# Row-reversing copies of two outputs in a single-core forward and backward kernel: three large DMAs against sixteen small ones

## The chip, the cores and the metric

The kernel runs on one core of one Trainium2 chip. The metric is device time in microseconds (us) of one launch, forward and backward together. A core has a matrix engine (TensorE, PE in the profile), VectorE (DVE), ScalarE (ACT), GpSimd (POOL) and SyncE (SP); each runs its own instructions in order, and DMAs are issued by SP, ACT or POOL and then run by themselves. An engine waits on semaphores, so an instruction that waits also holds up what stands behind it on its engine.

## The reference, cut to what matters

```python
def _fwd_reference(A_u, ..., B_w1, B_w3, B_w2):
    x  = A_u                                   # 1 x 2048 x 576, bf16
    xn = _layernorm(x)
    # s: a state-space convolution along the 2048 rows
    K  = einsum("dn,dnl,dn->dl", C, exp(dt * A * l), dt * B).real
    s  = irfft(rfft(xn, padded to 2L) * rfft(K, padded to 2L))[:L] + xn * Dskip
    # g: a gated MLP, width 4608
    g  = silu((silu(xn @ w1) * (xn @ w3)) @ w2)
    return x + s * g

def reference(..., grad_out):
    out, vjp = jax.vjp(_fwd_reference, ...)
    return (out, *vjp(grad_out))   # out, dA_u, eight gradients of the
                                   # state-space parameters, dw1, dw3, dw2
```

out_0 is `out` and out_1 is the gradient of A_u, each 2048 x 576 in bf16. out_10, out_11 and out_12 are the gradients of the three weight matrices.

## The kernel before, in words

**Token tiles.** The 2048 rows are worked in 16 tiles of 128 rows. The convolution is done with matrix products that play the part of Fourier transforms, and for these the odd tiles hold their rows in reversed order. `self.order` (in `backward`) lists the eight odd tiles first, then the eight even ones. A result of an even tile goes straight to its place in the output. A result of an odd tile goes to a scratch tensor in DRAM, `self.odd["out_0"]` or `self.odd["out_1"]`, 8 x 128 x 576 each, 1152 KB. From there DMAs from DRAM to DRAM copy it to the output with the rows turned round again; the helper `turned` (L173) gives the access pattern of the odd rows of an output in reversed order.

**Stages around the change.** The forward stage ends with the stores of out_0 and of its odd tiles (L1152). Then `ssm_bwd_conv` (L1183) runs the backward of the convolution in four quarters (`conv_bwd_quarter`), interleaved with the weight gradients of the MLP. These are worked in 18 groups of 256 columns: `backward` loops over `gi` and takes each group's generator, `phase6_group` (L1724), stage by stage. In a group, matmuls L1746 make `ph`, ACT casts it to `gh` (L1749), DVE multiplies `gu_n` and `gg_n` by it (L1764), SP stores both to `GU_dram` and `GG_dram` (L1769, two halves each), and L1807 to L1822 make the gradients of w1 and w3, which POOL stores (L1792, L1813). ACT's Silu and its derivative for the next group are L1713 and L1717, with DVE's products L1720 and L1721. Stages named "out_11_0" to "out_10_1" are steps of the gradient part, "stored" comes right behind the stores.

In a convolution quarter, SP loads spectra (L86: `a` from `UH_dram` and `KH_dram`, `az` likewise), DVE multiplies them with `g` to `Z` and `ZZ` (L867 to L876, L1319, L1324), TensorE turns these back (L841, L851), ACT evicts `gds_sb` and `gk_st` (L1332, L1337, L1340), and SP stores them (L1334, L1344).

**The last stage** (`phase6_inputs`) runs over the 16 tiles in `self.order`, i = 0 to 15. For each, SP loads transposed activations `acts` from `GU_dram` and `GG_dram` (L1669), TensorE multiplies them with the weights (`px`, L1857), and `ln_bwd_tile` and `ln_finish` do the backward of the layer norm (L1896 to L1931) and store the tile. Between these, the parameter gradients take `gz` and `pz` (L1376, L1379) and a transposed `qT` (L1669, from `Q_dram`) through matmuls L1389, DVE's product `pr_q` (L1394) and its sum (L1397).

**What sets the order.** The program is written as generators with due times: `self.at(T)` sets a priority, and a scheduler then arranges each engine's instructions by these priorities and by an estimate of when operands are ready. `issue_after(x)` makes an instruction be issued behind x. The helper `self.sp` keeps a class of SP's DMAs in the order in which they are written. So a moved DMA can also move instructions of other engines.

**The copies.** out_0 is one DMA of 8 x 128 x 576 on SP's queue at L1200, due at `T0 + 60`. out_1 is two DMAs of 4 x 128 x 576 on POOL's queue at L1934, written behind the finish of tiles i = 10 and i = 13, and set by the scheduler at 1553 and 1645 us of the profiled execution.

Of the kernel before, what the change touches and what calls it, by code (L numbers as in the profile page):

```python
# [100 lines left out]
class K:  # L101
# [71 lines left out]
    def turned(self, ap, t0=0, t1=None):  # L173
        rows = ap.rearrange("(i two p) d -> two i p d", two=2, p=P)[1]
        return rows[t0:t1, ::-1]

    def tok(self, name, t):
        ap = self.aps[name].flatten_outer_dims()
# [1004 lines left out]
    def ssm_bwd_conv(self, T0, TQ, ps):  # L1183
        nc, cfg = self.nc, self.cfg
        D, LT = cfg.D, cfg.LT
        self.gK_dram = self.dram.tile([4, P // 2, D // 64, 2, 2, 2, 8 * LT], BF16, name="gK_dram")
        with self.pool(name="b_g", bufs=1, side="right") as self.bgp, \
                self.pool(name="b_k", bufs=1, side="right") as kp, self.pool(name="b_z", bufs=2, side="right") as zp:
            self.at(T0)
            self.lcol = kp.tile([P, LT], FP32, name="lcol")  # L1190
            nc.vector.tensor_scalar(out=self.lcol[:], in0=self.irow[:, 0:LT], scalar1=float(P),
                                    scalar2=self.pcol[:, 0:1], op0=ALU.mult, op1=ALU.add)
            nc.vector.tensor_scalar(out=self.lcol[:], in0=self.lcol[:], scalar1=1.0 / 512, scalar2=None, op0=ALU.mult)
            self.at(T0 - 100)
            self.dft_turn_sines()
            self.cCS = kp.tile([P, 2, 2, cfg.LS], BF16, name="cCSb")
            with self.tc.issue_after(self.hc_loads[5].ins):
                nc.sync.dma_start(out=self.cCS[:], in_=self.CS_dram[:].rearrange("m i p k -> p m i k"))
            self.at(T0 + 60)
            nc.sync.dma_start(out=self.turned(self.aps["out_0"].flatten_outer_dims()), in_=self.odd["out_0"][:])  # L1200
            for g in range(4):
                yield from self.conv_bwd_quarter(g, kp, zp, ps, T0 + g * TQ, TQ)

# [306 lines left out]
    def backward(self, T0, TG, TQ, TC, TX, gctx, mats):  # L1510
        nc, cfg = self.nc, self.cfg
# [11 lines left out]
        with ExitStack() as out:  # L1523
# [60 lines left out]
            for gi in range(NG):  # L1584
                self.chain = gi >= GP
                lastg = gi == NG - 1
                nxt = self.phase6_load(gi + 1, T0 + TG * gi, TG, wp, inp) if not lastg else None
                prep = nxt[-1] if nxt else iter(())
                if lastg:
                    self.tail()  # L1590
                self.at(T0 + TG * gi)
                hs[gi] = cur[1]
                w2 = lambda g, fl: self.phase6_grad2(g, fl, hs[g], gwp, ps_gw)
                for stage in group if gi == 0 else self.phase6_group(gi, cur, elp, gwp, ps_h, ps_gw):
                    if stage == "h3" and self.chain and gi + 2 < NG:
                        self.w2Ts[gi + 2] = self.phase6_load_w2(gi + 2, wp)
                    if stage in ("h2", "h3", "out_11_0", "out_11_1", "out_11_2", "out_11_3", "out_10_0", "out_10_1"):
                        next(prep, None)
                    if stage in ("h1", "h3"):
                        if gi < NG - 1:  # L1600
                            w2(gi, stage == "h3")
                        if stage == "h3" and gi + 2 < NG:
                            self.phase6_load_h(gi + 2, T0 + TG * gi, inp)
                    if stage == "out_11" and gi == NG - 2:
                        self.load_piece(wT, inp, "h_n", 1, 22, 7)
                    if stage == "h1" and lastg:
                        self.load_piece(wT, inp, "gg_n", 0, 15, 7)
                        self.load_piece(wT, inp, "gu_n", 1, 15, 7)
                        self.load_piece(wT, wp, "w2T", 1, 13, 2)
                    if stage == "end" and 0 <= gi - GP < cfg.DT:  # L1610
                        for part in wT[0:2]:
                            self.load_wT_rows(part, gi - GP)
                    if stage == "stored":
                        c = gi - GP
                        if c in (1, 2, 3, 4):
                            step()
                        if lastg:
                            self.hold = []
                            self.phase5_turn()
                            acts = [self.load_acts(0)]  # L1620
                            for fl in range(2):
                                w2(gi, fl)
                                step()
                                self.phase5_step(self.half // 2)
                                self.phase5_step(self.half // 2)
                            acts.append(self.load_acts(1))
                            self.ready = sum(part[2] for part in wT)
                            self.load_piece(wT, wp, "w2T", 1, 11, 2)
                            self.load_piece(wT, inp, "h_n", 0, 22, 7)
                    elif stage in ("h1", "h3", "out_11", "out_10", "end") and gi >= GP and not (lastg and stage in ("out_10", "end")):  # L1630
                        step()
                        if lastg and stage == "out_11":
                            self.phase5_step(self.half // 2)
                            self.phase5_step(self.half // 2)
                cur = nxt
# [88 lines left out]
    def phase6_group(self, gi, tiles, elp, gwp, ps_h, ps_gw):  # L1724
        nc, cfg = self.nc, self.cfg
        D, LT, FG = cfg.D, cfg.LT, self.FG
        nfull = D // P
        LH = LT // 2
        w2T, hn, gg, gu = tiles[0:4]
        pair = lambda t_: t_[:].rearrange("p (j t) f -> p j t f", j=2)  # L1730
        made = {}

        def make(s):
            if gi == 0 and s == 3:
                gh = gwp.tile([P, 2, 2, FG], BF16, name="gh_3", tag="gw13")
            else:
                gh = elp.tile([P, 2, 2, FG], BF16, name="gh6")
            ph = [ps_h.tile([P, 2, FG], FP32, name="ph") for _ in range(2)]
            for k in range(2):
                t = s * 2 + k  # L1740
                for j in range(2):
                    tt = j * LH + t
                    steps = [(self.goT[:, c, tt * P:(tt + 1) * P], w2T[:, :, c, :]) for c in range(nfull)]
                    steps.append((self.goTt[:, tt * P:(tt + 1) * P], w2T[:, :, nfull, :]))
                    for n, (lw, rh) in enumerate(steps):
                        self.pe_last = nc.tensor.matmul(ph[j][:, k, :].rearrange("p (a f) -> p a f", f=P), lhsT=lw, rhs=rh,  # L1746
                                                        start=(n == 0), stop=(n == nfull))
            for j in range(2):
                self.sc(lambda: nc.scalar.copy(out=gh[:, j], in_=ph[j][:]))  # L1749
            made[s] = gh  # L1750

        if gi == 0:
            make(0)
            yield "open"
            for s in range(1, 4):
                make(s)
                yield "early"
        for s in range(LH // 2):
            if s not in made:
                make(s)  # L1760
            gh = made[s]
            sl = slice(s * 2, s * 2 + 2)
            for t_ in (gu, gg):
                nc.vector.tensor_tensor(out=pair(t_)[:, :, sl], in0=gh[:], in1=pair(t_)[:, :, sl], op=ALU.mult)  # L1764
            yield f"h{s}"
        for (dst, t_) in ((self.GU_dram, gu), (self.GG_dram, gg)):
            for j in range(2):
                ts = slice(j * LH, (j + 1) * LH)
                self.sp(lambda: nc.sync.dma_start(out=dst[ts, :, gi * FG:(gi + 1) * FG].rearrange("t p f -> p t f"),  # L1769
                                                  in_=t_[:, ts, :]))  # L1770
        yield "stored"
        yield from self.phase6_grad13(gi, gg, gu, gwp, ps_gw)

# [153 lines left out]
    def ln_finish(self):  # L1927
# [1 line left out]
        self.nc.vector.scalar_tensor_tensor(out=o1, in0=gx[:], scalar=self.rstd[:, t:t + 1], in1=gs[:],  # L1929
                                            op0=ALU.mult, op1=ALU.add)  # L1930
        self.nc.scalar.dma_start(out=self.tok("out_1", t), in_=o1)  # L1931
        if i in (10, 13):
            q = slice(0, 4) if i == 10 else slice(4, 8)
            self.nc.gpsimd.dma_start(out=self.turned(self.aps["out_1"].flatten_outer_dims(), q.start, q.stop), in_=self.odd["out_1"][q])  # L1934


# [99 lines left out]
```

## Time and profile before

| | us |
|---|---|
| median of 3 runs | 1788.87 (1781.19 to 1794.86) |
| the profiled execution | 1793.5 |
| its span | 1791.7 |
| TensorE busy | 1664.5 (93%) |
| VectorE busy | 1358.6 (76%) |
| ScalarE busy | 912.5 (51%) |
| GpSimd busy | 347.1 (19%) |
| mean granted clock of TensorE | 0.988 |

The span runs from the first to the last recorded instruction; the time lies 1.8 us above it. Line numbers (L1200) are those of the kernel before. A row of a timeline gives the start, the duration, the engine, the line, the operation, the tiles out<-in, and in brackets the idle time of the engine before it and what ended it. A row of waits gives the engine and the tile that waited, the line, what it waited for, the time in total, how often, and the longest. SPq and POOLq are the DMA queues' own rows.

### The profile page before, as it was taken

What the parts mean: (1) busy time and instruction counts of PE and PEld (TensorE: products, weight loads), DVE (VectorE), ACT (ScalarE), POOL (GpSimd) and SP (SyncE); (2) the same over time, 40 slices, a digit from 0 to 9 for tenths busy, and PEclk for the clock granted to TensorE, in tenths of its full rate; (3) what the DMA queues carried; (4) which work ended last, traced back from release to release, by engine and by line L of the source; (5) the groups of instructions that cost most, each with busy time, mean ns of one, the idle gap of its engine ahead of it and who ended that gap; (6) DMA issues with size and microseconds to landing.
All of it is one profiled execution on the core that took longest, in us unless ns stands there. A gap on an engine that the chain in (4) does not pass through costs nothing. (4 is left out here: it accounts for less than half of the span.)

```text
span 1791.7 us, 38769 instructions
## 1 busy us (share of the span) xinstructions
PE 1664.5 (93%) x15637; PEld 1228.2 (69%) x15637; DVE 1358.6 (76%) x2102; ACT 912.5 (51%) x1649; POOL 347.1 (19%) x565
## 2 busy tenths in 40 slices
PE   7789999999999999989999999999999987989997
PEld 3455555554545777777888888888888765768875
DVE  8768888887692555858978889659999955858675
ACT  6778888886864112764666666564445410101001
POOL 3112222213134111101111111111111233131032
PEclk9999999999999999999999999999999999999999
DMA  7789999889698989748666756589999999999992
GB/s 225 266 271 343 321 343 316 297 271 275 212 294 245 233 195 196 219 145 238 190 179 206 202 174 191 158 221 275 247 262 241 220 232 235 211 212 225 233 240 48
DMA packets 635483, 416.90 MB, mean 233 GB/s; under 512 B 424407, under 2 KB 575943, under 8 KB 630695
## 3 DMA queue, kind: packets, MB, share of 16 engines
q1 hardware_dynamic: 579620, 287.34, 64.5%
q0 software_dynamic: 31904, 106.81, 18.2%
q10 hardware_dynamic: 23778, 20.28, 4.2%
q8 instruction: 122, 2.00, 0.5%
q14 instruction: 59, 0.48, 0.1%
HBM read 135.60 MB, written 190.89 MB: 182 GB/s over the span
## 5 line engine op out<-in xcount | busy, mean ns | idle before, releaser
L1857 PEld LDWEIGHTS <-acts 128*128 128x128 bf16 x2304 | 224.9, 98 | 75.2 <-DMA acts<-GU_dram 11.4
L1807 PEld LDWEIGHTS <-xn_bf 128*128 128x128 bf16 x2304 | 224.5, 98 | 44.6 <-issue 18.4
L1394 DVE TENSOR_TENSOR pr_q<-et_ps,pz 128x1024 f32<-128x1024 f32 x144 | 176.0, 1222 | 29.5 <-PE et_ps L1389 14.8
L1857 PE MATMUL px<-wT,acts 128*128 128x288 bf16 x1472 | 191.6, 288 | 1.5 <-DMA wT<-in_B_w_dram 1.5
L1746 PE MATMUL ph<-w2T,goT 128*128 128x256 bf16 x1440 | 176.2, 275 | 8.7 <-ACT gh L1749 8.5
L1025 PEld LDWEIGHTS <-xnT 128*128 128x128 bf16 x1152 | 107.0, 98 | 109.2 <-issue 18.3
L1397 DVE TENSOR_REDUCE S_all<-pr_q 128x32 f32<-128x1024 f32 x144 | 175.3, 1217 | 3.1
L1746 PEld LDWEIGHTS <-goT 128*128 128x128 bf16 x1440 | 140.4, 99 | 28.8 <-issue 11.4
L1025 PE MATMUL pg<-wmB_w,xnT 128*128 128x512 bf16 x576 | 154.0, 380 | 2.1 <-ACT g_t L1041 1.8
L1025 PE MATMUL pu<-wmB_w,xnT 128*128 128x512 bf16 x576 | 154.3, 379 | 0.0
L1787 PE MATMUL pgw<-go_o,h_n 128*128 128x288 bf16 x1152 | 149.0, 286 | 0.2
L1807 PE MATMUL pgw<-gu_n,xn_bf 128*128 128x256 bf16 x1152 | 135.2, 273 | 10.4 <-ACT gw L1791 5.5
L1787 PEld LDWEIGHTS <-h_n 128*128 128x128 bf16 x1152 | 112.3, 98 | 30.0 <-issue 2.0
L1807 PE MATMUL pgw<-gg_n,xn_bf 128*128 128x256 bf16 x1152 | 130.5, 272 | 2.4 <-ACT gw L1809 2.3
L1809 ACT CAST gw<-pgw 128x256 bf16<-128x256 f32 x144 | 52.3, 374 | 144.6 <-PE pgw L1807 144.5
L1039 ACT ACTIVATE s_t<-pg 128x512 bf16<-128x512 f32 x144 | 87.8, 610 | 74.0 <-PE pu L1033 36.2
L1857 PE MATMUL px<-wA,acts 128*128 128x288 bf16 x832 | 110.5, 288 | 15.7 <-DMA acts<-GU_dram 10.5
L674 ACT ACTIVATE cs_k<-et_ps 128x512 bf16<-128x512 int16 x216 | 111.5, 630 | 0.1
L1749 ACT CAST gh<-ph 128x512 bf16<-128x512 f32 x144 | 81.3, 600 | 54.9 <-PE ph L1746 54.9
L1913 ACT ACTIVATE go<-gx 128x576 bf16<-128x576 f32 x16 | 10.9, 684 | 193.1 <-DVE gx L1896 109.4
L1053 POOL DMA_DIRECT2D G_dram<-g_t x72 | 52.4, 727 | 285.0 <-DVE g_t L1043 146.4
L1044 ACT CAST u_t<-pu 128x512 bf16<-128x512 f32 x144 | 87.4, 607 | 7.6 <-PE pu L1025 7.5
(316 smaller groups left out, 3206.0 us busy)
## 6 DMA issues: line engine op xcount, KB each, us to landing
U_dram<-u_t POOLq DMA_DIRECT2D x72, 256.0 KB, 5.3
G_dram<-g_t POOLq DMA_DIRECT2D x72, 256.0 KB, 4.7
H_dram<-h_t SPq DMA_DIRECT2D x72, 256.0 KB, 4.0
Q_dram<-q_k SPq DMA_DIRECT2D x36, 512.0 KB, 4.7
gg_n<-G_dram POOLq DMA_DIRECT2D x18, 1024.0 KB, 6.7
h_n<-U_dram POOLq DMA_DIRECT2D x18, 1024.0 KB, 8.6
GU_dram<-gu_n SPq DMA_DIRECT2D x36, 512.0 KB, 4.3
GG_dram<-gg_n SPq DMA_DIRECT2D x36, 512.0 KB, 10.5
```

What stands on the lines that cost most here:

```text
L674: self.sin_last = nc.scalar.activation(out=CS[:, :, o:o + 256], in_=pt[:].bitcast(I16)[:, :, 0::2], func=ACT.Sin, scale=6.283184 / 2 ** 16)
L1025: ins = nc.tensor.matmul(pt[:], lhsT=xnT[:, c, ts], rhs=wm[w][:, c, :], start=(q == 0 and c == 0), stop=(q == 1 and c == nfull - 1))
L1039: nc.scalar.activation(out=s_t[:, :, q, :], in_=pgv, func=ACT.Silu)
L1044: nc.scalar.copy(out=u_t[:, :, q, :], in_=puv)
L1053: self.u_stores[step] = nc.gpsimd.dma_start(out=dst[fb * ng:(fb + 1) * ng, :, i0:i0 + NT, :].rearrange("g p t f -> p g (t f)"), in_=src[:] ...
L1394: nc.vector.tensor_tensor(out=pr[:].rearrange("p r k e -> p r (k e)"), in0=T[h][:].rearrange("p k z d a -> p (k z d a)")[:, None].to_broad ...
L1397: nc.vector.tensor_reduce(out=self.S_all[:, :, d0:d0 + 4], in_=pr[:].rearrange("p r k (d a) -> p (r k) d a", d=4), op=ALU.add, axis=AX.X)
L1746: self.pe_last = nc.tensor.matmul(ph[j][:, k, :].rearrange("p (a f) -> p a f", f=P), lhsT=lw, rhs=rh, start=(n == 0), stop=(n == nfull))
L1749: self.sc(lambda: nc.scalar.copy(out=gh[:, j], in_=ph[j][:]))
L1787: self.pe_last = nc.tensor.matmul(pgw[pi_][:, 0:pw], lhsT=hn[:, tt, fl * P:(fl + 1) * P], rhs=go_o[:, tt, po:po + pw], start=(tt == 0), st ...
L1807: self.pe_last = nc.tensor.matmul(pw_[:, 0:FG], lhsT=self.xn_bf[:, tt, c * P:(c + 1) * P], rhs=nat[:, tt, :], start=(tt == 0), stop=(tt == ...
L1857: self.pe_last = nc.tensor.matmul(px[pi_][:, 0:pw], lhsT=acts[i][:, ai, fi, :], rhs=w[:, po:po + pw], start=(n == 0), stop=(n == len(steps ...
```

## The change

Both outputs' copies are cut into eight parts of 16 rows of each of the eight odd tiles (8 x 16 x 576, 144 KB). The out_0 copy leaves `ssm_bwd_conv`; its parts are issued by SP in the groups gi = 2 to 9 at stage "out_11_2", behind the group's last store of `GG_dram`. The out_1 copies are issued by POOL, two in each `ln_finish` of i = 10 to 13. The bytes stay the same, the DMAs go from 3 to 16. Since a part touches all eight odd tiles, each of the out_1 copies needs all eight odd stores.

```diff
+    def turn_out(self, k):
+        sl = slice(16 * k, 16 * k + 16)
+        with self.tc.issue_after(self.gg_store.ins):
+            self.nc.sync.dma_start(out=self.turned(self.aps["out_0"].flatten_outer_dims())[:, sl],
+                                   in_=self.odd["out_0"][:, sl])
...
                 nc.sync.dma_start(out=self.cCS[:], in_=self.CS_dram[:].rearrange("m i p k -> p m i k"))
-            self.at(T0 + 60)
-            nc.sync.dma_start(out=self.turned(self.aps["out_0"].flatten_outer_dims()), in_=self.odd["out_0"][:])
             for g in range(4):
...
+                    if stage == "out_11_2" and 0 <= gi - 2 < 8:
+                        self.turn_out(gi - 2)
                     if stage == "stored":
...
-                self.sp(lambda: nc.sync.dma_start(out=dst[ts, :, gi * FG:(gi + 1) * FG].rearrange("t p f -> p t f"),
-                                                  in_=t_[:, ts, :]))
+                self.gg_store = self.sp(lambda: nc.sync.dma_start(
+                    out=dst[ts, :, gi * FG:(gi + 1) * FG].rearrange("t p f -> p t f"), in_=t_[:, ts, :]))
...
-        if i in (10, 13):
-            q = slice(0, 4) if i == 10 else slice(4, 8)
-            self.nc.gpsimd.dma_start(out=self.turned(self.aps["out_1"].flatten_outer_dims(), q.start, q.stop), in_=self.odd["out_1"][q])
+        if i in (10, 11, 12, 13):
+            for k in range(2 * i - 20, 2 * i - 18):
+                sl = slice(16 * k, 16 * k + 16)
+                self.nc.gpsimd.dma_start(out=self.turned(self.aps["out_1"].flatten_outer_dims())[:, sl],
+                                         in_=self.odd["out_1"][:, sl])
```

`self.at(T0 + 60)` acts on nothing else: the quarters that follow set priorities of their own. The scheduler's order changes in two places. Around groups 0 to 3, SP's gds store, ACT's eviction of gds and gk, TensorE's L841 and DVE's products with the KH spectra stand at other places; in the last stage small blocks of L1389 and the POOL copies do. Elsewhere each engine's order is as before.

## The prediction

> **What bounds the kernel now.** I read the page first, then TensorE's busy time by stretches, the waits inside the two stretches with gaps, and SP's timeline there.
>
> ```profile
> span 1791.7 us, 38769 instructions
> PE 1664.5 (93%) x15637; PEld 1228.2 (69%) x15637; DVE 1358.6 (76%) x2102; ACT 912.5 (51%) x1649; POOL 347.1 (19%) x565
> ```
>
> TensorE is busy 93% of the span, so a transfer costs time only where it leaves TensorE without work. Some 127 us are without; the question is which of them the copies touch. The busy time by stretches (columns: stretch, its length, then PE, PE weight loads, DVE, ACT, POOL, the granted clock, the DMA share, GB/s):
>
> ```profile
> 780.00:790.00 10.00, 5.30 (x61) 4.61 (x59) 1.45 (x4) 6.72 (x11) 0.00 (x0) 0.88 0.15 41
> 790.00:800.00 10.00, 9.06 (x65) 7.08 (x65) 2.71 (x5) 7.74 (x13) 1.08 (x2) 0.78 0.90 236
> 800.00:820.00 20.00, 15.89 (x156) 13.69 (x154) 14.88 (x28) 5.80 (x13) 3.15 (x5) 0.87 1.08 330
> 820.00:840.00 20.00, 20.00 (x176) 16.92 (x175) 19.04 (x35) 12.95 (x20) 1.65 (x3) 0.96 0.60 139
> 1570.00:1580.00 10.00, 5.01 (x28) 3.55 (x29) 3.89 (x4) 0.00 (x0) 3.25 (x8) 0.66 1.10 228
> 1640.00:1650.00 10.00, 10.00 (x89) 8.08 (x87) 9.56 (x10) 0.00 (x0) 1.18 (x1) 1.00 1.07 248
> ```
>
> Two gaps lie near the copies: 780 to 820, just behind the out_0 copy (issued at 730.14), and 1570 to 1580, just behind the first out_1 copy. The second out_1 copy (1644.89) falls where TensorE is full: it costs nothing. Who waits in the gaps, 780 to 810 and 1560 to 1585:
>
> ```profile
> DVE gu_n L1764 <- ACT gh L1749: 9.6, 1, 9.6
> ACT gds_sb L1332 <- PE et_ps L841: 6.5, 1, 6.5
> DVE gg_n L1720 <- ACT gg_n L1717: 6.2, 1, 6.2
> PE ph L1746 <- ACT gh L1749: 5.3, 1, 5.3
> DVE Z L867 <- DMA a<-KH_dram: 5.0, 1, 5.0
> ...
> PE et_ps L1389 <- DMA gz<-gK_dram: 6.6, 1, 6.6
> ```
>
> And what SP issued (start, duration):
>
> ```profile
> 783.55 0.69 SPq L1334 DMA_DIRECT2D out_dram<-gds_sb  x1
> ...
> 797.88 5.80 SPq L86 DMA_DIRECT2D a<-KH_dram  x1
> ...
> 1551.08 8.73 SPq L1669 DMA_TRANSPOSE acts<-GU_dram  x1
> 1559.90 10.55 SPq L1669 DMA_TRANSPOSE qT<-Q_dram  x1
> 1570.51 1.23 SPq L1376 DMA_DIRECT2D gz<-gK_dram  x2
> ```
>
> **Gap 1 is a matter of order.** ACT stands 6.5 us at L1332 until TensorE ends the 32 matmuls L841 (784.1). It then does six evictions L1337/L1340, a table load and two Silu passes before the casts L1749 (790.0) that TensorE needs. DVE waits 9.6 us for the same cast. SP has stood at the gds store L1334 for 33.4 us, so the KH loads behind it leave at 797.9, and DVE waits for them until 808.7.
>
> TensorE's work from 784.05 to 821.06 at the rate of undisturbed rows: 40 matmuls L1746 and 128 of L1807 at 0.112 us (64 of L1807 take 7.15) are 18.8; 32 of L1817/L1819 run from 809.0 to 810.8, 1.8; 32 of L851, 16 in 1.16, about 2.1. That is 22.7 of 37.0: 14.3 us lost. At a clock of 0.96 another 0.8 goes in 820 to 840. Together 15.1.
>
> **Part 1: the out_0 copy.** It leaves SP's queue (0.76 us, and 4.9 of waiting for the last odd_out store); no engine waits for its landing, so taking it away gains nothing by itself. But the scheduler builds another order without it. On SP the gds store goes behind the KH and KHz loads of the next quarter and the w2 loads. On ACT the gds cast and six evictions go behind the Silu, gh, derivative and first gw casts. On TensorE 7 of the 32 L841 run first, then L1807, with the rest of L841 strewn between, and L1746 afterwards. On DVE the Z products that needed the KH loads come forward. So the four long waits above lose their cause. What I expect to stay: 1 to 2 us near 783 while ZZ is made, and 3 to 4 while ACT's evictions free et_ps for the strewn L841 (six of them took 3.5 us). 15.1 less 5 gives **10.1**. Bounds: 15.1, all of it; 0, when the strewn matmuls meet a new wait as long. I take the value near the upper end, because each released wait shows its releaser in a row.
>
> **Part 2: eight copies of 144 KB on SP**, each right behind the four stores GU/GG of groups 2 to 9, ahead of the next a/az loads. Issue: 0.35 to 0.45 us each by SP's rows of stores, 3 us in all, in a queue that waits most of the time. What they delay are the loads behind them. The rows 1551.08 and 1559.90 tell what a 576 KB copy on another queue does to SP's transposes: 8.73 for a median of 5.96 and 10.55 for one of 2.88, together 10.4 us; a quarter of the bytes, 2.6. The least slack I found from an a load's landing to its use is about 3.6 us (loads of 883 to 888, used at 897.5); between quarters it is about 10. So 2.6 is covered: **0**. Bound without cover: 8 x 2.6 = 21 us. Below nothing isn't reached: no wait between 830 and 1170 has a DMA as its releaser on a compute engine.
>
> By the Trainium skill (DMA: Bandwidth & Descriptors, "Why a DMA increments its semaphore by 16 and not by 1") a transfer is spread over as many engines, 16 at most, as divide its slowest dimension: the 4x128x576 copies would lie on 4 engines and the new 8x16x576 ones on 8. An estimate by it is an eighth of the load on each engine, 1.3 us a copy in place of 2.6; no row shows the spread.
>
> **Part 3: the first out_1 copy leaves 1553.** Its rows:
>
> ```profile
> 1553.07 1.18 POOL L1934 DMA_DIRECT2D out_dram<-odd_out  x1 [4.45 <-DMA odd_out<-go]
> ...
> DMA to landing us min/median/max: 12.2/15.0/17.9
> ```
>
> While it flies the acts and qT transposes take the 10.4 us more; gz, queued behind qT, is issued at 1570.5 in place of about 1560, and TensorE waits 6.61 us at L1389. The slowed clock (0.66) then stretches 30 matmuls L1857 to 5.65 us, 3.84 elsewhere, and eight of L1389 to 1.01, 0.61 elsewhere. 6.61 + 1.81 + 0.40 = **8.8 us**, all of it on the path. In the changed order POOL issues no copy until tile 10, so this goes. Bounds: 8.8; 0, if SP is late there for another reason.
>
> **Part 4: eight out_1 copies of 144 KB at tiles 10 to 13**, all touching all odd tiles, so the first still waits for the last odd store (1639 plus landing, as the second copy does now, 6.46 us of POOL at 1644). POOL's issues of 128 rows cost 0.55 to 0.77 us; the clump is three in a row, about 2 us, ahead of sc and gxs (L1921 to L1924). ACT's even stores gain no wait. SP's waits from 1580 to 1760:
>
> ```profile
> SPq L1669 <- PE et_ps L1389: 43.6, 14, 6.1
> SPq L1669 <- PE px L1857: 37.5, 8, 10.8
> ```
>
> SP stands 81 us of 180 waiting for TensorE to free buffers: that is the cover. Between 1640 and 1660 one acts transpose already takes 12.74 us against a median of 5.68, and TensorE stays at 10.00. The same bytes fly now within some 50 us: 10.4 for each 576 KB is 20.8 us against 81: **0**. Without cover: one stall as at 1575 for every two copies, 4 x 8.8 = 35.
>
> **Sum.** 1793.5 (the profiled execution, span 1791.7) - 10.1 - 8.8 = 1774.6. That execution lies 4.6 us above the median of the runs; the gain of 18.9 off the median 1788.87 gives **1770.0**.
>
> **Rivals.**
> *Only one gain comes.* Gap 1 moves rather than closes (for it: the strewn L841 need et_ps buffers that ACT frees late; against: DVE and SP get their work earlier): 1788.9 - 8.8 = 1780.1. Or gap 2 stays since the transposes are slow anyway (for it: DMA share above 1 there; against: medians of 5.96 and 2.88): 1788.9 - 10.1 = 1778.8.
> *It does nothing it seems to:* the copies were hidden before, no one waits for their landing, and both gaps come back elsewhere in the new order: 1789. For it, L1200 has no waiter; against it, gap 2's chain of rows.
> *Slower: the copies hold up the a/az loads of the gradient groups.* They enter SP's queue between 2 MB of stores and these loads; the first a load there already takes 5.09 to 6.11 us to issue. If a copy costs as much as a slow 144 KB landing, 5.9 us, it passes the slack of 3.6 by 2.3 at each of eight groups; with the slow clock after a stall (2.2, as at 1575) that is 8 x 4.5 = 36 us. With gap 1 lasting for the same lateness of KH, only 8.8 comes back: 1788.9 + 36 - 8.8 = 1816. It decides from 3.6 us a copy on.
> The Trainium skill (the same page, "Anatomy of one DMA — SWDGE (gpsimd) path") speaks for this side: about 2.0 us fixed for each such DMA. Three DMAs becoming sixteen would be 26 us by it were they in a line on the path; the trace has nobody waiting for a copy's landing.
>
> **How the numbers follow.** A measurement here tells about 1% (17.9 us, 1771.0) from no change. Both gains: 0.60, of which I put 0.43 beyond 1% and 0.17 within, since 18.9 is hardly above the bound. One gain: 0.11, of which 0.02 beyond, if the other comes in part. Nothing: 0.07. Slower: 0.22. So faster 0.45, same 0.33, slower 0.22. The likeliest case's own range: 15.1 + 8.8 gained gives 1765, and the runs scatter by 6 to 8 us: 1758 to 1782. The range to be held reaches towards the slower case without its centre: 1758 to 1804.
>
> **What would show it.** Right: no wait of 5.3 us at L1746 near 785; KH loads issued before 780; DVE without its idle 9.6, 6.2 and 5.0; the granted clock near 1 from 780 to 840; no wait for gz near 1570, a qT transpose of about 3 us there; copies L1934 from about 1640 on with TensorE at 10 of 10. Wrong: waits on a<-KH_dram or a<-UH_dram between 830 and 1170, L841 waiting for ACT, POOL's gxs late behind copies, or a new gz/qT wait from 1640 to 1700.

## The result, and the profile after

The changed kernel ran at a median of 1784.15 us (1773.82 to 1813.63, 20 runs), the kernel before at 1802.68 us (1781.19 to 1826.84, 20 runs). The ratio is 0.9933, with a 95% interval of 0.9905 to 0.9961: about 12 us faster, 7 to 17. It is the figure to go by: the medians lie 18.5 us apart, which would look like the forecast, but they hold disturbed, slower runs as well, and the ratio does not. The forecast of 1770.0 against 1788.87 was a ratio of 0.9895, just outside that interval: the sign was right and the gain, 18.9 us, too large. The profiled executions differ by 11.8 us of span.

The page of the changed kernel, first lines:

```profile
span 1779.9 us, 38735 instructions
PE 1653.7 (93%) x15573; PEld 1226.6 (69%) x15637; DVE 1357.8 (76%) x2102; ACT 912.4 (51%) x1649; POOL 348.5 (20%) x571
```

The share of TensorE is the same 93%; what was gained is invisible there and shows only by stretches (columns as before):

```profile
780.00:790.00 10.00, 9.16 (x84) 7.62 (x82) 9.86 (x18) 8.21 (x13) 1.08 (x2) 1.00 0.71 193
790.00:800.00 10.00, 9.99 (x102) 8.80 (x101) 6.27 (x11) 3.63 (x8) 0.99 (x2) 1.00 0.71 229
800.00:820.00 20.00, 18.25 (x197) 15.93 (x194) 15.47 (x30) 10.39 (x21) 2.71 (x5) 1.00 0.71 195
...
1570.00:1580.00 10.00, 10.00 (x89) 8.08 (x87) 8.80 (x19) 0.40 (x1) 6.01 (x10) 1.00 1.25 247
1580.00:1590.00 10.00, 8.03 (x73) 6.45 (x71) 2.63 (x6) 1.64 (x3) 5.45 (x11) 1.00 1.11 246
...
1640.00:1650.00 10.00, 10.00 (x90) 8.10 (x89) 6.10 (x7) 1.06 (x3) 3.56 (x6) 1.00 1.14 218
```

Gap 1 is closed but for the 2 us of 800 to 820, and the granted clock is 1.00 throughout, as foretold. Gap 2 at 1570 is closed too, but a new, smaller one of 2 us stands at 1580 to 1590. SP's rows show the new order that was foretold: the KH loads leave 30 us earlier than the 797.88 of before, ahead of the gds store.

```profile
768.08 0.34 SPq L86 DMA_DIRECT2D a<-KH_dram  x1
...
801.57 0.72 SPq L1338 DMA_DIRECT2D out_dram<-gds_sb  x1
```

In the last stage qT takes 2.54 us where it took 10.55, and TensorE's wait there has another releaser:

```profile
1553.36 2.54 SPq L1675 DMA_TRANSPOSE qT<-Q_dram  x1
```

```profile
1588.60 0.82 DVE L1935 SCALAR_TENSOR_TENSOR go<-gx,rstd,gxs 128x576 bf16<-128x576 f32 x1 [7.34 <-POOL gxs L1930]
...
1590.60 0.38 PE L1393 MATMUL et_ps<-gz,qT 128*128 128x128 bf16 x4 [2.58 <-DVE pr_q L1398]
```

More has moved in the last stage than the small blocks of L1389 and the POOL copies: DVE's `go` (L1929 before) now stands right behind its tile's statistics, ahead of products `pr_q` that stood in front of it before, and POOL's `sc` and `gxs` (L1921 to L1924) have moved as well.

**Where the time goes, by landmarks.** The cast of gw13t (L1822 before, L1828 after) comes once per group, always behind the same work. Its rows for groups 1, 5, 12 and 18 of 18 mark off stretches that can be compared between executions, however they are shifted. Before, then after:

```profile
762.35 0.37 ACT L1822 CAST gw13t<-pgw 128x256 bf16<-128x256 f32 x1 [1.53 <-PE pgw L1819]
937.35 0.37 ACT L1822 CAST gw13t<-pgw 128x256 bf16<-128x256 f32 x1 [1.52 <-PE pgw L1819]
1220.28 0.37 ACT L1822 CAST gw13t<-pgw 128x256 bf16<-128x256 f32 x1 [1.52 <-PE pgw L1819]
1447.99 0.37 ACT L1822 CAST gw13t<-pgw 128x256 bf16<-128x256 f32 x1 [1.53 <-PE pgw L1819]
```

```profile
762.87 0.37 ACT L1828 CAST gw13t<-pgw 128x256 bf16<-128x256 f32 x1 [1.53 <-PE pgw L1825]
927.09 0.37 ACT L1828 CAST gw13t<-pgw 128x256 bf16<-128x256 f32 x1 [1.53 <-PE pgw L1825]
1209.99 0.37 ACT L1828 CAST gw13t<-pgw 128x256 bf16<-128x256 f32 x1 [1.53 <-PE pgw L1825]
1448.06 0.37 ACT L1828 CAST gw13t<-pgw 128x256 bf16<-128x256 f32 x1 [1.53 <-PE pgw L1825]
```

First stretch (around gap 1): 175.0 against 164.2 us, 10.8 less. Second (the out_0 parts): 282.9 against 282.9. Third: 227.7 against 238.1, 10.4 more, in a part of the program that the change leaves alone. From the last landmark to the span's end: 343.7 against 331.9, 11.8 less. So the 11.8 us of this pair are 10.8 of gap 1, and two large differences that nearly cancel. The experiments had to tell which of these come again.

### The profile page after: what moved, and what is told of

Same layout as the page of the kernel before. It is cut to its first block, busy times and chain, and to the rows that moved or that the text cites. A ratio compares the mean times of both kernels' runs of the same rounds, so it can differ in the third digit from the quotient of the medians.

```text
span 1779.9 us, 38735 instructions
## 1 busy us (share of the span) xinstructions
PE 1653.7 (93%) x15573; PEld 1226.6 (69%) x15637; DVE 1357.8 (76%) x2102; ACT 912.4 (51%) x1649; POOL 348.5 (20%) x571
## 3 DMA queue, kind: packets, MB, share of 16 engines
q0 software_dynamic: 31488, 106.80, 18.5%
## 5 line engine op out<-in xcount | busy, mean ns | idle before, releaser
L1031 PE MATMUL pg<-wmB_w,xnT 128*128 128x512 bf16 x526 | 144.3, 381 | 8.3 <-issue 5.8
## 6 DMA issues: line engine op xcount, KB each, us to landing
GG_dram<-gg_n SPq DMA_DIRECT2D x36, 512.0 KB, 10.2
```

The source lines that it names most:

```text
L1031: ins = nc.tensor.matmul(pt[:], lhsT=xnT[:, c, ts], rhs=wm[w][:, c, :], start=(q == 0 and c == 0), stop=(q == 1 and c == nfull - 1))
```

## The experiments

Theory 1: gap 1 goes because the scheduler's order changes, steadily; gap 2 goes too, in each execution; the parts cost nothing. The rivals are in the expectations. Below, "first stretch" and so on are the times between the same landmarks in each kernel's own trace.

**Each half alone.** e1 takes the changed kernel and puts the out_1 copies back:

```diff
-        if i in (10, 11, 12, 13):
-            for k in range(2 * i - 20, 2 * i - 18):
...
+        if i in (10, 13):
+            q = slice(0, 4) if i == 10 else slice(4, 8)
+            self.nc.gpsimd.dma_start(out=self.turned(self.aps["out_1"].flatten_outer_dims(), q.start, q.stop), in_=self.odd["out_1"][q])
```

> The out_0 part of the change alone (eight parts behind the groups' stores); out_1 is copied as before by two DMAs. Theory 1 (the gain of gap 1 is one of order and steady, and the middle copies cost nothing): ratio to before 0.994 (10 to 11 us of 1790), the rows of 780 to 840 as in the changed kernel, TensorE at 19 of 20 in 780 to 800; the last stage keeps the out_1 copy at about 1543 with a wait for gz of 5 to 7 us behind it. Rival A (the copies in the groups cost part of it): ratio 0.997 or more, with waits on a<-KH_dram or a<-UH_dram between 830 and 1170. Rival B (gap 2 of the kernel before was one execution's accident): same ratio as theory 1, but no gz wait of over 2 us behind the out_1 copy.

Measured: ratio 0.9912 (0.9874 to 0.9950). First stretch 164.3, second 282.9. No wait for gz of over 2 us behind the first copy (1540), so that sentence of theory 1 failed; instead TensorE met four short waits for acts behind the second copy (1617):

```profile
1641.42 3.85 PE L1863 MATMUL px<-wA,acts 128*128 128x288 bf16 x30 [1.80 <-DMA acts<-GG_dram]
...
1696.64 3.73 PE L1863 MATMUL px<-wA,acts 128*128 128x288 bf16 x17 [4.40 <-DMA acts<-GU_dram]
```

e2 is the kernel before with the same block the other way round, so the out_1 part alone.

> The out_1 part of the change alone (eight parts at tiles 10 to 13); out_0 is copied as before by one DMA. Theory 1 (gap 2 comes in each execution): ratio 0.995 (8.8 us), gap 1 stays as in the kernel before (TensorE at 14 to 15 of 20 in 780 to 800). Rival B (gap 2 comes in some executions only, and its mean is a few us): ratio 0.998 to 1.000. Rival C (the eight copies late in the last stage cost something of their own): ratio at or above 1.000 with a wait of TensorE between 1640 and 1700.

Measured: ratio 0.9985 (0.9951 to 1.0019). First stretch 173.8, gap 1 still there. The gain of the out_1 part is small or none: rival B. Rival C's wait between 1640 and 1700 isn't in its trace. So the whole of the change's gain that can be told from nothing lies in the out_0 part. By its time alone e2 doesn't exclude the forecast: its interval reaches from 3.4 us lost to 8.8 gained.

**Size or place.** e3 cuts the out_0 copy but leaves it where it was in the text:

```diff
             self.at(T0 + 60)
-            nc.sync.dma_start(out=self.turned(self.aps["out_0"].flatten_outer_dims()), in_=self.odd["out_0"][:])
+            for k in range(8):
+                sl = slice(16 * k, 16 * k + 16)
+                nc.sync.dma_start(out=self.turned(self.aps["out_0"].flatten_outer_dims())[:, sl], in_=self.odd["out_0"][:, sl])
```

> The kernel before with the out_0 copy cut into the eight 144 KB parts but left at its place in the text, ahead of the convolution quarters; out_1 as before. The order of TensorE and ACT comes out as in the changed kernel. Theory 1 (gap 1 goes because eight small DMAs make the scheduler build another order, wherever they are written): ratio 0.994, no wait of 5 us at the ph matmuls near 785. Rival D (the place counts: the copies behind the groups free SP's queue): ratio 0.998 or more, gap 1 still there.

Measured: ratio 0.9952 (0.9915 to 0.9989), first stretch 164.2, TensorE 19.15 of 20 in 780 to 800. From the first landmark to the second, TensorE and ACT go through their instructions in exactly the order of the changed kernel. The cut is enough; the place behind the groups' stores isn't needed, and rival D falls. The scheduler did spread the parts, though: SP issued five from 732.8 to 749.1 and the other three at 778.8, 793.5 and 794.2. The trace of this kernel also holds no wait of TensorE for a DMA of 0.9 us or more after 1545, with the out_1 copies where they were.

**The converse.** e5 copies out_0 by the eight parts in the groups, and puts one DMA of the old size at the old place, to a spare tensor:

```diff
+            spare = self.dram.tile([LT // 2, P, D], BF16, name="spare_odd")
+            self.at(T0 + 60)
+            nc.sync.dma_start(out=spare[:, ::-1], in_=self.odd["out_0"][:])
             for g in range(4):
```

> out_0 is copied by the eight parts behind the groups' stores, and besides a DMA of 1152 KB from the scratch tensor to a spare DRAM tensor stands where the out_0 copy stood; out_1 as before. The orders of TensorE, ACT and POOL are those of the kernel before, the copies' traffic in the groups is that of the changed kernel. Theory 1 (gap 1 is the order's): ratio 1.000, within 0.003, gap 1 back with TensorE at 14 to 15 of 20 in 780 to 800. Rival D (the copies' place brings the gain): ratio 0.994. Rival A (the copies in the groups cost time): ratio 1.003 to 1.012 with new waits between 830 and 1170.

Measured: ratio 0.9987 (0.9946 to 1.0027), first stretch 175.1. Gap 1 is back with all of its waits, though out_0 itself is copied as in the changed kernel:

```profile
DVE gu_n L1773 <- ACT gh L1758: 9.7, 1, 9.7
...
ACT gds_sb L1339 <- PE et_ps L847: 6.5, 1, 6.5
DVE gg_n L1729 <- ACT gg_n L1726: 6.3, 1, 6.3
...
PE ph L1755 <- ACT gh L1758: 5.3, 1, 5.3
DVE Z L873 <- DMA a<-KH_dram: 4.8, 1, 4.8
```

Against the lines of before: 9.6, 6.5, 6.2, 5.3, 5.0. TensorE's and ACT's order in the first stretch is exactly that of before. With e3 this shows the cause from both sides: one 1152 KB DMA at that place of the text, also when it goes to a spare tensor, makes the scheduler build the order with the gap, and eight of 144 KB make it build the other. The copy's own traffic is not the cause: in the first trace of the kernel before its 1024 packets of 1152 bytes are through at 741.4, some 40 us ahead of the gap. The second stretch of e5 is 282.9 again.

**What the parts cost in the groups.** e7 issues each twice:

```diff
                     if stage == "out_11_2" and 0 <= gi - 2 < 8:
                         self.turn_out(gi - 2)
+                        self.turn_out(gi - 2)
```

> The changed kernel with each of the eight out_0 parts issued twice in a row (the second writes the same rows again). TensorE's and ACT's orders are those of the changed kernel. Theory 1 (a part costs nothing in the groups): ratio 0.993, shift between 840 and 1280 unchanged. Rival A (a part beyond the slack of the a loads costs 2 to 4 us each): ratio 0.998 to 1.011, waits on a<-KH_dram or a<-UH_dram.

Measured: ratio 0.9876 (0.9830 to 0.9922), first stretch 164.2, second 282.9. Twice the parts cost nothing that TensorE sees; DVE waits 3.3 us in all for az loads from KHz_dram, which no stretch shows. The ratio lies under the expected 0.993; the changed kernel had 0.9922 (0.9885 to 0.9960, e8) in the same set, so the two can't be told apart. SP's rows at one group, of the kernel before and of the changed one, show how a part is covered:

```profile
880.08 2.89 SPq L1769 DMA_DIRECT2D GG_dram<-gg_n  x2
883.02 5.09 SPq L86 DMA_DIRECT2D a<-KH_dram  x1
```

```profile
869.70 2.90 SPq L1775 DMA_DIRECT2D GG_dram<-gg_n  x2
872.65 5.29 SPq L180 DMA_DIRECT2D out_dram<-odd_out  x1
877.99 0.83 SPq L86 DMA_DIRECT2D a<-KH_dram  x1
```

The DMA that comes next behind the stores is the one that is slow to issue, whichever it is: in the kernel before 5.1 to 6.1 us at four of the eight groups, for a, az and w2r loads. Before, it was the a load, 5.09 us; now it is the part, 5.29, and the a load behind it leaves in 0.83. From the start of the GG stores to the end of the first load's issue it was 8.0 us and is 9.1: here a part delays the loads by 1.1 us, and at the five other groups that can be compared by 0 to 0.7.

**No out_1 copies at all.** e6 drops the block from the changed kernel.

> The changed kernel without any copy of the odd rows of out_1 (they stay in the scratch tensor). TensorE's, ACT's and SP's orders are those of the changed kernel. Theory 1 (the copies at tiles 10 to 13 are hidden): the same time as the changed kernel, ratio to before 0.993. Rival C (they cost several us in the last stage): ratio 0.989 or less. Theory 2 (the stalls of the last stage come from slow transposes that fall at another place in each execution, and the copies only add to them): 0.990 to 0.993, and some stall of 1 to 6 us on acts, gz or qT between 1290 and 1540 stays.

Measured: ratio 0.9921 (0.9886 to 0.9956), the changed kernel's own. The last stretch is 334.8 us; with the eight parts it was 331.6 to 339.8 in five traces. The parts at tiles 10 to 13 cost nothing that stands out of this scatter, and the 2.7 us wait for pr_q at 1588 stays without them: it belongs to the order.

**How often the last stage's waits come.** e4 is the kernel before and e8 and e11 the changed kernel, unchanged, for more traces.

> The kernel before, unchanged, as a second sample of its trace and of the scatter. Every theory: ratio 1.000 within 0.003. Theory 1 says that both gaps are in this trace too: TensorE at 14 to 15 of 20 in 780 to 800, and a gz wait of 5 to 7 us near 1570. Rival B says that gap 2 is not, or at another size.

> The changed kernel, unchanged, as a second sample of its trace. Every theory: ratio 0.993 within 0.004. Theory 2: the stalls between 1290 and 1340 of the first trace (1.8, 3.3 and 5.2 us on gz) are not there again or at other places and sizes, gap 1 is closed by the same 10 to 11 us. Rival E (those stalls belong to the changed kernel and are what gives the gain of the last stage back): they are at the same places again, 8 to 12 us in all.

> The changed kernel, unchanged, a third sample. Ratio 0.9925 within 0.004 by every theory. Theory 2 (the 14 and 22 us that a pair of wA transposes took near 1290 in the two traces so far are accidents of an execution): such a pair takes 14 us or more in some traces and 7 to 8 in others, so in this one either; a trace of 7 to 8 settles that it isn't the kernel's own. Rival E (they belong to the changed kernel): again 14 us or more near 1290 and 8 to 16 us of waits from 1280 to 1400.

Measured: 0.9968 (0.9929 to 1.0008), 0.9922 (0.9885 to 0.9960) and 0.9896 (0.9833 to 0.9958). e4 is the kernel before against itself, so its 0.9968, just outside the expected 0.003, is a measure of what such a ratio can be off by. In e4 the wait of 6.61 us at 1575 isn't there; one for the same operand stands behind the other out_1 copy, which was the harmless one in the first trace:

```profile
1652.65 1.01 PE L1389 MATMUL et_ps<-gz,qT 128*128 128x128 bf16 x8 [5.41 <-DMA gz<-gK_dram]
```

Adding up TensorE's waits of 0.9 us and more from 1565 on: with the out_1 copies as before 9.8 us (first trace), 5.4 (e4), 12.7 (e1), 8.8 (e5) and 0 (e3), mean 7.3. With the eight parts 3.7 (first trace), 3.6 (e2), 2.6 (e8), 4.5 (e7) and 9.1 (e11), mean 4.7. Late copies have no wait for a DMA among them, but all have the one for pr_q at about 1590, 2.6 to 3.6 us and once 7.0:

```profile
1596.89 0.58 PE L1393 MATMUL et_ps<-gz,qT 128*128 128x128 bf16 x4 [7.02 <-DVE pr_q L1398]
```

So the part exchanges 7.3 for 4.7 us: some 2.6, not 8.8. Lengths say much the same: from TensorE's second block of four transposes of `ST` (L1471, at 1554.09 in the first trace, where the first old copy starts) to the span's end it is 237.6, 233.0, 242.3, 239.4 and 225.9 us with the old copies (order as above: first trace, e4, e1, e5, e3) and 229.8, 230.0, 230.3, 231.9 and 237.6 with the parts (first trace, e2, e8, e7, e11), 3.7 us less on the mean. Both agree with e2's ratio (2.7 us), whose interval is wide.

What repeats in every trace is that transposes beside the old copies are slow. In the five traces with these copies, from 85 to 300 us behind the last landmark, the eight transposes of acts from GG_dram that overlap a copy (from its issue to its landing) took 8.5 to 12.7 us, median 11.3, and the others 5.6; the six of qT took 5.0 to 15.4, median 6.9, and the others 2.7. What varies is whether TensorE then waits: 9.7 us for DMAs in e1, and none in e3, though two transposes took 10.4 and 12.4 us there. Presumably it depends on how far ahead SP is; no run varies that alone.

The third stretch is what scatters most: 227.7 (first trace), 228.3, 228.2 and 227.5 in four traces of kernels with the old out_1 copies and 227.7 in e7, but 233.8 in e3, 238.1, 246.2 and 237.8 in the three traces of the changed kernel, 241.4 in e2, and 230.7 to 236.5 in e6, e9 and e10. Where it is long, one pair of wA transposes on SP took 12 to 22 us in place of 6 to 10, and gz behind it came late; the place differs: near 1290 in the first trace and e8, near 1330 in e3, e2, e10 and e11, near 1380 in e9 (e6 has none). The first transpose of the pair near 1290 took 12.09 us in the changed kernel's first trace and 5.06 in e7.

e8 has waits on gz of 7.25 and 4.68 us at 1313 and 1342, about where the first trace had 3.25 and 5.16, as rival E said; e11 has 6.80 us for the pair near 1290 but a wait of 7.85 us at 1371. So the place isn't the changed kernel's own, but the length may be: all three of its traces are over 9 us longer here than the two of the kernel before. The order of every engine is the same there, and the out_1 copies come some 300 us later. Whether it is chance that long stretches came with late out_1 copies in most traces, and with the old ones in e3 alone, no run settles.

**Many or late.** e9 copies out_1 by two DMAs, but each of half the rows of all odd tiles; e10 is the same with the out_0 part of the change:

```diff
         if i in (10, 13):
-            q = slice(0, 4) if i == 10 else slice(4, 8)
-            self.nc.gpsimd.dma_start(out=self.turned(self.aps["out_1"].flatten_outer_dims(), q.start, q.stop), in_=self.odd["out_1"][q])
+            sl = slice(0, 64) if i == 10 else slice(64, 128)
+            self.nc.gpsimd.dma_start(out=self.turned(self.aps["out_1"].flatten_outer_dims())[:, sl], in_=self.odd["out_1"][:, sl])
```

> The kernel before with out_1 copied by two DMAs again, but each of 64 rows of all eight odd tiles, so that both need the last odd store; out_0 as before. Both stand late on POOL, behind tile 7's store, as the eight parts do. Theory 2 (what matters is where the first out_1 copy stands, not how many there are; the stalls on acts, gz and qT behind an early copy are 0 to 10 us, some 6 in the mean, and a new wait of DVE's pr_q takes back 3): ratio 0.995 to 0.999, no wait of TensorE for a DMA of over 2 us from 1545 to 1700. Rival F (small parts matter, a 576 KB copy makes such stalls wherever it stands): waits of 5 us or more on gz or acts behind 1640 and ratio 1.000.

> The out_0 part of the change with the out_1 copies of two DMAs of 64 rows of all odd tiles. Theory 2: as the changed kernel or a little under it, ratio 0.990 to 0.994, and 780 to 840 as in the changed kernel. Rival F: 0.995 or more.

Measured: e9 1.0001 (0.9958 to 1.0044), e10 0.9850 (0.9792 to 0.9908). Neither trace has a wait of TensorE for a DMA of 0.9 us or more from 1545 to 1700, and both have the one for pr_q (2.7 and 3.0). So small parts aren't needed, and rival F falls. A copy of four whole odd tiles is ready after the fourth store and is put at 1553; one that cuts across all tiles can't be issued before the eighth. But theory 2, by which the place of the first copy is what matters, isn't borne out either: in e4, e5 and e1 the waits stand behind the second old copy, issued at 1637.5, 1636.9 and 1617.2, and the copies of e9 and e10, at 1627.1 to 1657.9, have none. Beside the old form the transposes of acts from GG_dram took 8.5 to 12.7 us, beside the 64-row form 8.0 and 8.5. Form, place and the new order of the last stage were changed together, and no run parts them. As to the time, e9's 1.0001 against the expected 0.995 to 0.999 says again that the out_1 part is worth at most a few us. e10 is the lowest ratio of all, but in the same set the changed kernel (e11) had 0.9896 (0.9833 to 0.9958): the two can't be told apart.

## Why the prediction was right and wrong

- **Gap 1, 10.1 us: right, in size and cause.** The first stretch took 175.0, 174.2, 173.8, 175.1 and 174.2 us in five traces with the old order and 164.2 to 164.3 in eight with the new: 10.2 us on the mean, and the steadiest number of the study. The cause given, order and not traffic, is shown by e3 and e5. What the prediction did not see is that cutting alone does it. The size came out of bounds from 0 to 15.1 by an allowance of 5 us for what would stay, so that it is right to 0.1 us is luck. Of the 5 us expected to stay, TensorE's idle time from 780 to 840 in the changed kernel's first trace is 3.4 us, 1.5 of it from 800 to 805.
- **Part 2, nothing: right.** Second stretch 282.9 or 283.0 us in all traces, with parts, with doubled parts and without. The estimate of 2.6 us a part was too high (0 to 1.1), since the part takes over a wait that the load had. For the same reason its issue was put too low: 0.67 to 5.88 us each and 30 in all, where 0.35 to 0.45 and 3 had been expected, in a queue that had this time. The sentence that no compute engine waits for a DMA between 830 and 1170 overlooks one DVE wait of 1.6 us (gz, for GXN_dram); nothing hangs on it. The rival "slower" needed 3.6 us a part and falls.
- **Part 3, 8.8 us: the step that failed.** The chain behind the wait (copy, slow qT, late gz, TensorE) was read rightly, and transposes beside the old copies are slow in all five traces. But "all of it on the path" took one execution's wait for each execution's. With the old copies TensorE's waits for a DMA from 1565 on were 6.6, 5.4, 9.7, 8.8 and 0 us, mean 6.1, mostly behind the second copy, which the prediction called free; with the parts they were 0. And the term left out what the new order of the last stage brings: DVE's go waits for POOL's gxs (7.34 us at 1588), pr_q now stands behind go, and TensorE waits 2.6 us or more for the buffer. The waits for pr_q are 4.7 us on the mean with the parts and 1.2 with the old copies. Net some 2.6 us by the waits, 3.7 by the lengths, in place of 8.8.
- **Part 4, nothing: right**, as far as e6 can tell within the scatter of the last stretch.
- **The sum.** 10.2 + 2.6 is 12.8, against 12 measured; of the 6.9 us between forecast and result 6.2 are part 3. That these agree so well is luck in part: the three measurements of the same change gave 0.9933, 0.9922 and 0.9896, some 12, 14 and 19 us, and the sum leaves out the third stretch, 229.1 us on the mean with the old copies (five traces) and 238.2 with the parts (five), a difference which stays open. What tells against 8.8 us are the traces of the last stage, and e1, e2 and e9, not the total alone. Of the rivals, "only one gain comes" with gap 1 alone, 1778.8 or a ratio of 0.9944, was the nearest, and it had been given 0.11 where the full sum had 0.60.
- **The Trainium skill's two rules.** The fixed 2.0 us (DMA: Bandwidth & Descriptors, "Anatomy of one DMA — SWDGE (gpsimd) path") are given there for DMAs that POOL issues; only six of the thirteen more are, so the 26 us counted seven too many. As a price it didn't show: the second stretch, with five of SP's parts in it, with twice as many (e7) and with none, was 282.9 or 283.0 us, and nobody waits for the landing of these parts. On the spread over DMA engines, see the last section.

## What to carry to other kernels

Where a scheduler builds the order, cutting one big DMA can change the order of the compute engines (presumably through the scheduler's estimate of the DMA's time, which no run looked into); compare the orders of both kernels before asking what the transfer itself costs. Here the waits that repeated to 0.2 us from trace to trace belonged to the order and could be summed; the waits for a DMA in a busy queue came out as 0 to 9.7 us, and one trace gave one draw: count such a wait at a mean over executions or at a fraction. And look at what a moved block puts behind what: here a wait taken away upstream left a smaller one downstream.

## What the runs showed of the hardware

The same 576 KB from DRAM to DRAM, issued by POOL in the last stage, landed after 11.0 to 24.2 us in ten copies as 4 x 128 x 576, and after 7.1 to 8.2 us in four as 8 x 64 x 576. The view of the line's DMAs of e9:

```profile
L1934 POOL DMA_DIRECT2D out_dram<-odd_out x2: 870/890/911, 1643.7 to 1657.9; - x2
...
DMA to landing us min/median/max: 7.4/7.8/8.2
```

The transposes beside them followed: those of acts from GG_dram took 8.5 to 12.7 us (eight) beside the first form and 8.0 and 8.5 (two) beside the second, against 5.6 and 5.9 elsewhere in the same traces. The two forms were also issued at other moments, so the shape isn't shown to be the only cause. By the Trainium skill (DMA: Bandwidth & Descriptors, "Why a DMA increments its semaphore by 16 and not by 1") the first form lies on 4 engines and the second on 8. The medians, about 12 and 7.5 us, go that way, by a factor of some 1.6, though no row shows the spread itself.
